# ScalarE's part of a unit's maxima queued three slots later, and whole output units in the last steps of a fused attention and MLP kernel

## Chip, cores and metric

The kernel runs on one core of a Trainium2 chip. The metric is the device time in microseconds of one execution, as the median of several runs. Data is float32; most matrix products are done in float32r with the operands split into a high and a low part.

## What is computed

`x` has 2048 tokens of 576 channels. Two branches read it, and a gate per token mixes them:

```
H = 32; Dh = D // H                       # 18
q, k, v = split(x @ wqkv)
scores = einsum("bhqd,bhkd->bhqk", q, k) * Dh ** -0.5
a = (softmax(scores) @ v, heads joined) @ wo
y = layernorm(x)
b = gelu(y @ w1 + b1) @ w2 + b2           # 576 -> 4608 -> 576
g = sigmoid((x * gate_w).sum(-1))
out = g * a + (1 - g) * b
```

## The kernel before

The order of all instructions is written out by the program itself: a Python planner issues them one by one, each engine runs its own in that order, and semaphores hold an instruction back until its operands are there and its buffer is free.

**Stages.** First come layer norm, transposes and the projections to q, k and v (to about 250 us). Then a long loop does the attention and, between its steps, the MLP. At the end comes the output projection (`out_proj`, line 1297), which also mixes the branches.

**Attention.** A *unit* is a pair of heads and one half of the queries: 32 units. A unit takes 32 *rounds* and 16 *steps*. A round (`s1_round`, products at L227) computes a 128x512 block of scores for each of the two heads, and VectorE takes each row's maximum (L229). When the 32 rounds of a unit are issued, `s1_finish` reduces them to one negative maximum per query (`nm`, VectorE, L238); ScalarE splits it into a rounded part and the rest (`nmh` L239, `nm` L240, `nm2` L241); the function `rows` adds the rest on VectorE (L245), transposes (L246, tile `mr`), and eight small DMAs put the values as two more rows into the tile `qa` of the unit's queries. A step (`s2`) then does, for each half `qb` of the queries, a score product per head with the maximum already subtracted (L307, 56 rows of `qa` and `ka`), and ScalarE takes the exponential (L309, into `p` or `ring`). The two heads' products of a step go into two PSUM banks that only the exponentials free. Rounds have three PSUM banks that VectorE's maxima free in turn. Every second or third step `pv` multiplies the exponentials with v (L335), which closes a *cycle*. The rounds run about 20 steps ahead of the steps: a unit's rounds end four steps before its own first step.

**MLP.** A generator `mlp` yields after every pair of products. `h_pair` does one output of the first matrix (27 pairs of products, L578) and GELU; `out_pair` is one *output unit*: 24 pairs of products with w2 for 128 tokens (48 products, L710), added up on VectorE (L684). `atom` runs the generator up to the next cut that the unit itself has set (a third or so of an output unit), `stretch` for a given time. `fill` is called three times in a cycle of two steps and puts a piece of that work between the attention's products; its products share TensorE with those of a step, since each uses half of the array's rows (`weave`).

**Slots.** `run_due` ends each piece of issue. It counts slots; `defer(n, fn)` runs `fn` n slots later, and this is how small jobs are placed. A step has about four slots.

**Last steps.** The last 20 steps have no rounds left. There `fill` lets `stretch` run the rest of the MLP at a pace worked out from the steps left, and then starts the output projection, 8 products in a gap.

Of the kernel before, what the change touches and what calls it, by code (L numbers as in the profile page):

```python
# [9 lines left out]
F32 = mybir.dt.float32  # L10
F32R = mybir.dt.float32r
AF = mybir.ActivationFunctionType
# [31 lines left out]
GAP = 1130.0  # L44
TOTAL = NB * NG * (G // 2 * 27 * 231 + 8 * 3 * G * 131)
# [7 lines left out]
FIN = NSTEP - 6  # L53
# [7 lines left out]
def gated_mix_kernel(ctx: ExitStack, tc: tile.TileContext, x, wqkv, wo, w1, b1, w2, b2, gate_w, out):  # L61
    nc = tc.nc
# [69 lines left out]
    def dma_r(queue, dst, src):  # L132

        queue.dma_start(dst.bitcast(F32), src)
# [5 lines left out]
    def defer(n, fn):  # L140
        later.append((slot[0] + n, fn))
# [13 lines left out]
    def run_due(ns=SLOT):  # L155

        slot[0] += 1
        now[0] += ns
        if chain and chain[0][0]():
            chain.pop(0)[1]()  # L160
        due = [f for t, f in timed if t <= now[0]]
        timed[:] = [(t, f) for t, f in timed if t > now[0]]
        for f in due:
            f()
        due = [f for s, f in later if s <= slot[0]]
        later[:] = [(s, f) for s, f in later if s > slot[0]]
        for f in due:
            f()
        k = 0
        while k < len(bg):  # L170
            if pool_end[0] - now[0] < bg[k][2] and slot[0] >= bg[k][0]():
                bg.pop(k)[1]()
                k = 0
            else:
                k += 1
# [56 lines left out]
    def s1_finish(u):  # L232

        m4 = M4.pop(u)
        nm = asm.tile([P, 2, 2, 8], F32, name="nm")
        nm2 = asm.tile([P, 2, 2, 8], F32, name="nm2")
        nmh = asm.tile([P, 2, 8], F32R, name="nmh")
        nc.vector.tensor_reduce(nm[:, 0], m4, axis=AX.X, op=ALU.max, negate=True)  # L238
        nc.scalar.activation(nmh, nm[:, 0], AF.Copy)  # L239
        nc.scalar.activation(nm[:, 1], nmh.bitcast(F32), AF.Copy, scale=-1.0)  # L240
        nc.scalar.activation(nm2[:, :, 0, :], nmh.bitcast(F32), AF.Copy)  # L241

        def rows():
            mr = asm.tile([P, 32], F32, name="mr", bufs=1)
            nc.vector.tensor_reduce(nm2[:, :, 1, :], nm.rearrange("p k a b -> p a b k"), axis=AX.X, op=ALU.add)  # L245
            nc.vector.transpose(mr, nm2.rearrange("p a b c -> p (a b c)"))  # L246
            qa = QA[u % 3]
            aside = slot[0] < ybusy[0]

            def store(h, k):  # L250
                r = 64 * h + 54
                c = 32 * k + 16 * h
                dst = qa[r:r + 2, :].rearrange("b (t k n) -> b t k n", k=4, n=32)[:, :, k, :]
                dma_r(nc.scalar if aside else nc.sync, dst, mr[c:c + 16, :])
            for n in range(8):
                if aside:
                    defer(1 + n, lambda n=n: store(*divmod(n, 4)))
                else:
                    store(*divmod(n, 4))
        defer(2 if looped[0] else 8, rows)  # L260

    RING = []

# [105 lines left out]
    rounds = [(u, r) for u in range(NU) for r in range(NR)]  # L369
    rounds.reverse()  # L370

    looped = [False]

    def take_round():
        u, r = rounds.pop()
        head = s1_round(u, r)
        if r == NR - 1:
            defer(1, lambda: s1_finish(u))
        return head
# [425 lines left out]
    stream = [mlp()]  # L805
    spent = [0.0]
# [6 lines left out]
    def atom():  # L813

        while stream:
            try:
                spent[0] += next(stream[0])
            except StopIteration:
                stream.pop(0)
                return 0  # L820
            if cut[0]:
                end, cut[0] = cut[0], 0
                return end
        return 0

    def filler(upto):

        while stream and spent[0] < upto:
            try:
                spent[0] += next(stream[0])  # L830
            except StopIteration:
                stream.pop(0)
            end, cut[0] = cut[0], 0
            if end == 3:
                break
        run_due()


    def stretch(ns):

        upto = spent[0] + ns
        while stream and spent[0] < upto:
            try:
                spent[0] += next(stream[0])
            except StopIteration:
                stream.pop(0)
            end, cut[0] = cut[0], 0
            if end == 3:
                break
# [477 lines left out]
    base = spent[0]  # L1327
    proj = out_proj()
    over = [None]
    bare_at = []  # L1330
    opened = [False]
    at = [0]
    next(proj)
# [3 lines left out]
    def fill(step):  # L1337

        t = spent[0]
        gap = gaps[0]  # L1340
        gaps[0] += 1
        if over[0] is None and rounds:
            behind[0] = base + (TOTAL - KEPT - base) * step / BARE
            ended[0] = atom() == 2
            piece[0] += 1
            run_due(max(spent[0] - t, GAP))
        elif over[0] is None:
            if not bare_at:
                bare_at.extend((gap, spent[0], step))
            g0, s0, n0 = bare_at  # L1350
            stretch(s0 + (TOTAL - s0) * (gap + 1 - g0) / (1.5 * (FIN - n0)) - spent[0])
            run_due(max(spent[0] - t, GAP))
            if not stream:
                stream.append(proj)
                over[0] = gap - (spent[0] == t)
                spent[0] = 0.0
        if over[0] is not None and over[0] < gap:
            filler(PROJ * 122.5 * (gap - over[0]))
            run_due()
# [6 lines left out]
    for u in range(NU):  # L1366
        for kc in range(NT):
            step = u * NT + kc
# [21 lines left out]
            if step - done[0] >= room[0] or room[0] == 3 and ended[0] and step > done[0]:  # L1390
                pv(done[0], step)
                done[0] = step
                piece[0] = 0
                ended[0] = 0
                if extra[0]:
                    next_round()
                    extra[0] -= 1
            else:
                fill(step)
            s2(u, kc, 1, loop_round(), 462.0)  # L1400
            if not (room[0] == 3 and ended[0]):
                fill(step)
# [29 lines left out]
```

## Time and profile before

| | |
|---|---|
| median of 3 runs | 2273.99 us (2273.72 to 2274.64) |
| profiled execution | 2275.26 us |
| its span on the core | 2273.5 us |
| VectorE busy | 1657.7 us, 73% |
| ScalarE busy | 1442.2 us, 63% |
| GpSimd busy | 947.2 us, 42% |
| DMA | 323.62 MB, mean 142 GB/s |

The profile comes from one execution, which took 1.27 us more than the median. All times in it are counted from the start of the span. Each row of the timeline gives start, duration, engine, line, operation, tiles written and read, and in brackets the idle time of the engine before it and what ended that. PE is TensorE, DVE VectorE, ACT ScalarE, POOL GpSimd, SPq the queue of SyncE that issues DMAs. The measured ends of matrix products are modelled.

### The profile page before, as it was taken

Reading aid. Unit: us, or ns where it says so; the run is one execution under the profiler, and the core shown is the slowest. Engines: PE = TensorE matmul, PEld = TensorE weight load, DVE = VectorE, ACT = ScalarE, POOL = GpSimd, SP = SyncE. Lnnn points to the kernel's source line nnn. Section 1 sums busy time; section 2 is a strip of 40 time slices with the busy share of each in tenths; the row PEclk is TensorE's granted clock in tenths of the full one; section 3 lists DMA queues with packets and bytes.
Section 4 is the critical chain, followed back from the end, with each engine's and each line's share of the span. In section 5 each row is a group of like instructions: output and inputs, shape, how many; then the busy total and the mean of one; then the engine's idle time right before and its main releaser. Section 6 shows DMA issues by size and latency. Waiting matters only on the chain. (4 is left out here: it accounts for less than half of the span.)

```text
span 2273.5 us, 51161 instructions
## 1 busy us (share of the span) xinstructions
PE 2238.2 (98%) x20569; PEld 1628.6 (72%) x20569; DVE 1657.7 (73%) x2887; ACT 1442.2 (63%) x2719; POOL 947.2 (42%) x936
## 2 busy tenths in 40 slices
PE   8999999999999999999999999999999999999999
PEld 7878777776777677677667667677766776777669
DVE  5675777777777777777777777777777777777725
ACT  4223777777766666666666666666766666666761
POOL 4002466665654444444444444444624444433510
PEclk9999999999999999999999999999999999999999
DMA  7755645535464434332363323243554332333345
GB/s 242 258 188 182 196 158 157 165 134 189 154 179 181 121 119 121 98 118 98 115 171 127 118 98 121 98 149 111 142 181 128 110 119 93 99 99 112 95 157 192
DMA packets 163411, 323.62 MB, mean 142 GB/s; under 512 B 59838, under 2 KB 86370, under 8 KB 152338
## 3 DMA queue, kind: packets, MB, share of 16 engines
q1 hardware_dynamic: 159174, 313.57, 43.2%
q10 hardware_dynamic: 4000, 6.78, 0.8%
q8 instruction: 162, 2.65, 0.5%
q14 instruction: 75, 0.61, 0.1%
HBM read 229.07 MB, written 95.16 MB: 143 GB/s over the span
## 5 line engine op out<-in xcount | busy, mean ns | idle before, releaser
L229 DVE TENSOR_REDUCE m<-ps 128x1 f32<-128x512 f32 x2048 | 1302.9, 684 | 348.1 <-PE ps L227 310.2
L309 ACT ACTIVATE p<-ps 128x512 f32<-128x512 f32 x1080 | 587.4, 596 | 298.1 <-PE ps L227 193.8
L307 PE MATMUL ps<-qa,ka 56*128 56x512 f32 x2048 | 709.8, 413 | 18.9 <-ACT ring L309 15.2
L309 ACT ACTIVATE ring<-ps 128x512 f32<-128x512 f32 x968 | 525.4, 595 | 263.4 <-PE ps L227 202.2
L227 PE MATMUL ps<-ka,qa 54*128 54x512 f32 x2048 | 649.6, 417 | 3.6 <-DVE m L229 2.5
L710 PE MATMUL ps<-w,hh 64*128 64x288 f32 x4352 | 530.1, 297 | 0.7 <-ACT z L603 0.6
L307 PEld LDWEIGHTS ps<-qa,ka 56*128 56x128 f32 x2048 | 362.8, 185 | 234.5 <-issue 82.1
L578 PE MATMUL ps<-big,w 64*128 64x512 f32 x3888 | 517.4, 392 | 0.1
L180 POOL TENSOR_SCALAR zz<-zz 128x512 f32<-128x512 f32 x272 | 168.3, 619 | 779.9 <-ACT zz L666 749.8
L578 PEld LDWEIGHTS ps<-big,w 64*128 64x128 f32 x3888 | 379.8, 185 | 74.7 <-ACT vt L1016 0.3
L710 PEld LDWEIGHTS ps<-w,hh 64*128 64x128 f32 x4352 | 417.6, 186 | 14.5 <-ACT z L603 1.0
L180 POOL TENSOR_TENSOR zz<-zz,z 128x512 f32<-128x512 f32 x280 | 361.1, 1290 | 34.9 <-ACT zz L668 10.5
L227 PEld LDWEIGHTS ps<-ka,qa 54*128 54x128 f32 x2048 | 339.0, 186 | 34.5 <-DVE m L229 9.4
L710 PE MATMUL ps<-w,hl 64*128 64x288 f32 x2176 | 356.6, 293 | 0.0
L335 PE MATMUL ps<-p,vt 128*32 128x512 f32 x2160 | 266.1, 599 | 0.0
L710 PEld LDWEIGHTS ps<-w,hl 64*128 64x128 f32 x2176 | 241.4, 186 | 1.1
L335 PE MATMUL ps<-ring,vt 128*32 128x512 f32 x1936 | 238.8, 599 | 0.0
L180 POOL TENSOR_TENSOR w<-x,w 128x576 fp32r<-128x576 f32 (+1 forms) x34 | 68.3, 2011 | 282.6 <-ACT w L472 282.5
L180 POOL TENSOR_TENSOR hl<-zz,hh 128x512 fp32r<-128x512 f32 x134 | 174.2, 1300 | 15.3 <-ACT hh L629 4.5
L684 DVE SCALAR_TENSOR_TENSOR x<-ps,x 128x288 f32<-128x288 f32 x268 | 110.1, 452 | 95.4 <-PE ps L710 95.3
L335 PEld LDWEIGHTS ps<-p,vt 128*32 128x32 f32 x2160 | 57.9, 109 | 125.9 <-issue 124.7
L335 PEld LDWEIGHTS ps<-ring,vt 128*32 128x32 f32 x1936 | 52.2, 109 | 112.9 <-issue 112.9
(120 smaller groups left out, 1474.2 us busy)
## 6 DMA issues: line engine op xcount, KB each, us to landing
w<-w_scr SPq DMA_DIRECT2D x54, 1152.0 KB
w<-w_scr SPq DMA_DIRECT2D x108, 576.0 KB
w_scr<-w SPq DMA_DIRECT2D x18, 1152.0 KB
w_scr<-w SPq DMA_DIRECT2D x36, 576.0 KB
qa<-qk_scr SPq DMA_DIRECT2D x192, 72.0 KB
ka<-qk_scr SPq DMA_DIRECT2D x90, 144.0 KB
big<-y_scr SPq DMA_DIRECT2D x48, 256.0 KB
x<-in_B_w_dram SPq DMA_DIRECT2D x34, 288.0 KB
```

The costliest lines, as they stand in the source:

```text
L180: fn(*args, **kw)
L227: nc.tensor.matmul(ps, qa[r0:r0 + 54, t * P:(t + 1) * P], ka[r0:r0 + 54, kb * TB:(kb + 1) * TB], start=True, stop=True)
L229: nc.vector.tensor_reduce(M4[u][:, h, t, kb:kb + 1], ps, axis=AX.X, op=ALU.max)
L307: nc.tensor.matmul(ps, ka[r0:r0 + 56, kc * P:(kc + 1) * P], qa[r0:r0 + 56, qb * TB:(qb + 1) * TB], start=True, stop=True)
L309: nc.scalar.activation(ring(n)[:, qb, h], ps, AF.Exp, scale=SCALE)
L335: nc.tensor.matmul(OB[u][r:r + 32, :], v[:, k, 19 * h:19 * h + 32], ring(c)[:, qb, h, :], start=(k == 0), stop=(k == NT - 1))
L578: nc.tensor.matmul(ps[h], wt[w_][r, c, :], Y[s_][r, c, :], start=(k == 0), stop=(k == 26))
L684: nc.vector.scalar_tensor_tensor(dst, ps[nn][:, :ND], 0.5, b2b[:, cs[nn]] if base else dst, op0=ALU.mult, op1=ALU.add)
L710: mm = nc.tensor.matmul(ps[nn][:, :ND], h_[r, tok], w_[p_][r, cs[nn]], start=(k == 0 or bare and k == 3 * G), stop=(k == 6 * G - 1 or bare ...
```

## The change

There are two parts. In `s1_finish` ScalarE's three instructions go into a function `parts`, which runs three slots later (two before the loop has begun), and `rows` follows it at the distance that it had from `s1_finish` before. In `fill` the branch for steps without rounds goes: while the MLP has work left, every gap takes one piece by `atom`, as in the rest of the loop.

```
         nc.vector.tensor_reduce(nm[:, 0], m4, axis=AX.X, op=ALU.max, negate=True)
-        nc.scalar.activation(nmh, nm[:, 0], AF.Copy)
-        nc.scalar.activation(nm[:, 1], nmh.bitcast(F32), AF.Copy, scale=-1.0)
-        nc.scalar.activation(nm2[:, :, 0, :], nmh.bitcast(F32), AF.Copy)
+
+        def parts():
+            nc.scalar.activation(nmh, nm[:, 0], AF.Copy)
+            nc.scalar.activation(nm[:, 1], nmh.bitcast(F32), AF.Copy, scale=-1.0)
+            nc.scalar.activation(nm2[:, :, 0, :], nmh.bitcast(F32), AF.Copy)
+            defer(2 if looped[0] else 8, rows)
...
-        defer(2 if looped[0] else 8, rows)
+        defer(3 if looped[0] else 2, parts)
...
-        if over[0] is None and rounds:
+        if over[0] is None and stream:
             behind[0] = base + (TOTAL - KEPT - base) * step / BARE
             ended[0] = atom() == 2
             piece[0] += 1
             run_due(max(spent[0] - t, GAP))
-        elif over[0] is None:
-            if not bare_at:
-                bare_at.extend((gap, spent[0], step))
-            g0, s0, n0 = bare_at
-            stretch(s0 + (TOTAL - s0) * (gap + 1 - g0) / (1.5 * (FIN - n0)) - spent[0])
-            run_due(max(spent[0] - t, GAP))
-            if not stream:
-                stream.append(proj)
-                over[0] = gap - (spent[0] == t)
-                spent[0] = 0.0
+        if over[0] is None and not stream:
+            stream.append(proj)
+            over[0] = gap - (spent[0] == t)
+            spent[0] = 0.0
```

No instruction is added or removed. The lines behind the change shift: L307, L309 and L1297 of the program before are L310, L312 and L1300 of the changed one.

ScalarE, at the end of the rounds of unit 26 (near 1844 us), before: `nmh`, `nm`, `nm2` stand behind the exponentials of one step and ahead of the next pair.

```order
L659 ACTIVATE zz<-zz 128x512
L309 ACTIVATE p<-ps 128x512 x8
L309 ACTIVATE ring_2271<-ps 128x512 x4
L309 ACTIVATE ring_2279<-ps 128x512 x2
L239 ACTIVATE nmh<-nm 128x16
L240 ACTIVATE nm<-nmh 128x16
L241 ACTIVATE nm_26835<-nmh 128x2x8
L309 ACTIVATE ring_2279<-ps 128x512 x2
L309 ACTIVATE p<-ps 128x512 x8
```

The same place of the changed program:

```order
L662 ACTIVATE zz<-zz 128x512
L312 ACTIVATE p<-ps 128x512 x8
L312 ACTIVATE ring_2271<-ps 128x512 x4
L312 ACTIVATE ring_2279<-ps 128x512 x4
L312 ACTIVATE p<-ps 128x512 x2
L241 ACTIVATE nmh<-nm 128x16
L242 ACTIVATE nm<-nmh 128x16
L243 ACTIVATE nm_26835<-nmh 128x2x8
L312 ACTIVATE p<-ps 128x512 x6
```

The three instructions have moved behind two more pairs of exponentials.

VectorE at the same place, before: the two instructions of `rows` stand behind the sums of an output unit (L684) and ahead of all eight maxima (L229) of the next cycle.

```order
L684 SCALAR_TENSOR_TENSOR x<-ps,x 128x288 x2
L229 TENSOR_REDUCE m_25952<-ps 128x1 x8
L238 TENSOR_REDUCE nm<-m_25952 128x16
L684 SCALAR_TENSOR_TENSOR x<-ps,x 128x288 x2
L245 TENSOR_REDUCE nm_26835<-nm 128x2x8
L246 STREAM_TRANSPOSE mr<-nm_26835 128x32
L229 TENSOR_REDUCE m_26878<-ps 128x1 x8
L684 SCALAR_TENSOR_TENSOR x<-ps,x 128x288 x2
```

And changed:

```order
L229 TENSOR_REDUCE m_25938<-ps 128x1 x8
L238 TENSOR_REDUCE nm<-m_25938 128x16
L687 SCALAR_TENSOR_TENSOR x<-ps,x 128x288 x2
L229 TENSOR_REDUCE m_26864<-ps 128x1 x4
L248 TENSOR_REDUCE nm_26835<-nm 128x2x8
L249 STREAM_TRANSPOSE mr<-nm_26835 128x32
L229 TENSOR_REDUCE m_26864<-ps 128x1 x4
L687 SCALAR_TENSOR_TENSOR x<-ps,x 128x288 x2
```

`rows` has moved into the middle of the eight maxima.

TensorE in the last cycle of the loop, before, between the last two products with v (L335): products of a step (L307) and of the output projection (L1297).

```order
L335 MATMUL ps<-p,vt_115 32x512 x4
L307 MATMUL ps<-qa_110,ka_28066 128x512 x2
L1297 MATMUL ps<-big 128x288
L1297 MATMUL ps<-wlast,big 128x288
L1297 MATMUL ps<-big 128x288 x6
L307 MATMUL ps<-qa_110,ka_28066 128x512 x2
L1297 MATMUL ps<-big 128x288 x4
L1297 MATMUL ps<-wlast,big 128x288
L1297 MATMUL ps<-big 128x288 x2
L1297 MATMUL ps<-wlast,big 128x288
L307 MATMUL ps<-qa_110,ka_28066 128x512 x2
L1297 MATMUL ps<-big 128x288 x8
```

And changed:

```order
L338 MATMUL ps<-p,vt_115 32x512 x4
L310 MATMUL ps<-qa_110,ka_28066 128x512
L1300 MATMUL ps<-big 128x288
L310 MATMUL ps<-qa_110,ka_28066 128x512
L1300 MATMUL ps<-big 128x288 x7
L310 MATMUL ps<-qa_110,ka_28066 128x512
L1300 MATMUL ps<-wlast,big 128x288
L1300 MATMUL ps<-big 128x288
L310 MATMUL ps<-qa_110,ka_28066 128x512
L1300 MATMUL ps<-big 128x288
L1300 MATMUL ps<-wlast,big 128x288
L1300 MATMUL ps<-big 128x288 x4
```

The two products of a step, which stood together, now have a product or two of the projection between them. Over the cycles without rounds the 288 products of output units that are left come as 40, 40, 42, 40, 40, 40, 40 and 6 to a cycle before, in gaps of 12 or 14, and as 48 in each of six cycles now, in gaps of 14, 16 and 18. Of the 448 products of the projection 64 stand ahead of the last products with v before, in eight gaps (four of them divide a step's pair), and 96 now, in twelve gaps (eight of them divide it).

More of the change, by code (lines that the diff above doesn't have):

```diff
@@ L1329, in gated_mix_kernel @@
     over = [None]
-    bare_at = []
     opened = [False]
```

## The prediction

> **What bounds the kernel now.** I read the page first, then the waits of TensorE in the loop, then the timeline around one of them, then busy time by cycle. On the page the last column of a group is idle time and what ended it.
>
> ```profile
> span 2273.5 us, 51161 instructions
> PE 2238.2 (98%) x20569; PEld 1628.6 (72%) x20569; DVE 1657.7 (73%) x2887; ACT 1442.2 (63%) x2719; POOL 947.2 (42%) x936
> ```
>
> TensorE is busy 98% of the span, so a gain has to come out of its idle time or of products that run slower than they could. Who made it wait between 300 and 2140 us (total, times, longest), and one row of the same view for the whole span:
>
> ```profile
> PE ps L307 <- ACT ring L309: 13.7, 17, 0.8
> PE ps L307 <- ACT p L309: 2.1, 3, 0.8
> ACT nmh L239 <- DVE nm L238: 37.0, 31, 1.7
> ```
>
> Nearly all of it is one kind of wait: a step's product waits for the exponential that frees its bank, 17 times at 0.81 us, and in the second row twice at 0.80 (the third is 0.51). ScalarE in turn waits 31 times, up to 1.7 us, for the maxima of a unit. The timeline at the end of unit 26's rounds ties the two together:
>
> ```profile
> 1840.03 3.88 DVE L229 TENSOR_REDUCE m<-ps 128x1 f32<-128x512 f32 x6 [0.77 <-PE ps L227]
> 1842.87 0.39 PE L307 MATMUL ps<-qa,ka 56*128 56x512 f32 x1
> 1843.94 0.22 DVE L238 TENSOR_REDUCE nm<-m 128x16 f32<-128x64 f32 x1
> 1844.19 0.22 ACT L239 ACTIVATE nmh<-nm 128x16 fp32r<-128x16 f32 x1 [1.72 <-DVE nm L238]
> 1844.67 1.06 ACT L309 ACTIVATE ring<-ps 128x512 f32<-128x512 f32 x2
> 1845.30 0.49 PE L307 MATMUL ps<-qa,ka 56*128 56x512 f32 x1 [0.81 <-ACT ring L309]
> ```
>
> VectorE has six maxima in a row and reaches `nm` at 1843.94. ScalarE stands at `nmh` all that time, and the exponentials of the products of 1842.87, which were ready at about 1843.3, wait behind it until 1844.67. So the next product, 1845.30, waits. What that costs is more than the idle 0.81 us; three cycles with the same products (82 or 83 recorded), each from product with v to product with v, show it, the middle one with the wait:
>
> ```profile
> 1830.31:1837.60 7.29, 7.29 (x83) 5.47 (x81) 5.79 (x11) 4.41 (x10) 6.60 (x7) 1.00 0.03 13
> 1837.60:1846.22 8.62, 7.80 (x83) 5.71 (x81) 6.98 (x16) 5.01 (x12) 0.00 (x0) 1.00 0.01 3
> 1846.22:1853.51 7.29, 7.29 (x82) 5.47 (x81) 5.21 (x9) 4.13 (x9) 0.00 (x0) 1.00 0.14 46
> ```
>
> 8.62 less 7.29 is 1.33 us per unit, and the next cycle gives nothing back.
>
> **The change part by part.** *The wait goes.* `nmh` now comes after two more pairs of exponentials, which places it over the products with v. There ScalarE is idle, as before the first exponentials of the next cycle:
>
> ```profile
> 1846.22 0.64 PE L335 MATMUL ps<-ring,vt 128*32 128x512 f32 x4
> 1848.60 1.09 ACT L309 ACTIVATE p<-ps 128x512 f32<-128x512 f32 x2 [1.68 <-PE ps L227]
> ```
>
> ScalarE's three instructions take 0.48 us from the start of the first to the next exponential (1844.19 to 1844.67) and fit into 1.68, so I cost them at nothing; without that cover each unit would pay up to 0.48. `nm` has then been ready for over 2 us. Gain: 17 + 2 = 19 waits x 1.33 = 25.3 us. The other units end where TensorE did not wait, and give nothing.
>
> *`rows` moves into the maxima.* What is late next is VectorE. The price of `rows` is seen at unit 0, the new place at the cycle after unit 26:
>
> ```profile
> 243.38 0.17 DVE L245 TENSOR_REDUCE nm<-nm 128x16 f32<-128x32 f32 x1
> 243.66 0.21 DVE L246 STREAM_TRANSPOSE mr<-nm 128x32 f32<-128x32 f32 x1
> 243.81 1.29 DVE L229 TENSOR_REDUCE m<-ps 128x1 f32<-128x512 f32 x2
> 1848.64 3.88 DVE L229 TENSOR_REDUCE m<-ps 128x1 f32<-128x512 f32 x6 [1.34 <-PE ps L227]
> 1850.04 1.29 DVE L229 TENSOR_REDUCE m<-ps 128x1 f32<-128x512 f32 x2
> 1850.71 0.58 PE L227 MATMUL ps<-ka,qa 54*128 54x512 f32 x2
> ```
>
> `rows` takes 0.43 us (243.38 to 243.81). It now stands ahead of the third of these six maxima, which starts at 1850.04 and ends near 1850.73 (684 ns). The sixth product of the cycle, the second of the pair at 1850.71, reuses that maximum's bank and starts within 0.1 us of its end: it has no slack. Six maxima in 3.88 us are 0.64 apart, the second starts near 1849.25, VectorE could take the next instruction near 1849.86, and waits about 0.2 us for the third's product. So 0.43 less some 0.2 reach TensorE: I take 0.25 us. It may be 0 where there is more room, and 0.43 with none. The order shows this place at the 19 units above and at four more (2, 9, 16, 23): 23 x 0.25 = 5.8 us lost, between 0 and 9.9.
>
> *Unit 0.* Its `rows` come two slots later, and there the stores are already waited for:
>
> ```profile
> 243.90 5.42 SPq L134 DMA_DIRECT2D qa<-mr  x8
> 250.46 0.79 PE L307 MATMUL ps<-qa,ka 56*128 56x512 f32 x1 [0.70 <-DMA qa<-mr]
> ```
>
> Eight slots lay between 239.06 (its `nm`) and 243.66, some 0.6 us each, and the instructions passed are a pair of maxima, 1.3 us. The wait grows by that: 1.4 us lost, from 0 to 3.
>
> *Stores later in the other units.* The eight stores go out some three slots (a quarter of the step's 7.29 / 2 us each, 2.7 us in all) later. At unit 23, with little room and a load of weights that now goes ahead of them:
>
> ```profile
> 1662.16 5.30 SPq L134 DMA_DIRECT2D qa<-mr  x8
> 1667.56 0.34 SPq L134 DMA_DIRECT2D w<-w_scr  x1
> 1674.83 0.40 PE L307 MATMUL ps<-qa,ka 56*128 56x512 f32 x1
> ```
>
> From the last issue (1667.46) to the first use (1674.83) are 7.4 us; less 2.7 and a landing of 1.1 (unit 0: 249.32 to 250.46) leaves 3.6. Cost nothing; the load's issue takes 0.34 us and waits for nothing in this trace.
>
> *The last steps.* Rows: products with v from the chain of waits, the cycle with 40 output products, a wait and the granted clock (next to last but two) behind it.
>
> ```profile
> 2173.69:2180.11 6.42, 4.01 (x40) 3.42 (x40) 1.00 0.14 53
> 2149.79 0.49 PE L307 MATMUL ps<-qa,ka 56*128 56x512 f32 x1 [1.47 <-ACT ring L309]
> 2152.00:2154.00 2.00, 2.00 (x13) 0.56 (x16) 1.95 (x4) 1.34 (x3) 0.00 (x0) 0.50 0.90 364
> 2142.92 0.64 PE L335 MATMUL ps<-ring,vt 128*32 128x512 f32 x4
> 2152.20 3.24 PE ps L335 x16
> 2160.21 1.85 PE ps L335 x16
> 2200.93 1.85 PE ps L335 x16
> 2210.11 1.85 PE ps L335 x16
> 2217.03 1.85 PE ps L335 x16
> 2218.88 51.28 PE ps L1297 x384
> ```
>
> A cycle of 40 takes 6.42 us, though its output products fill only 4.01: ScalarE's eight exponentials (1.08 a pair) set its pace. Eight more products are four pairs; their price lies between 0, under the exponentials, and 8 x 4.01/40 = 0.80 us, on TensorE. I take 0: 6.4 us for 48. The first two cycles (2142.92 to 2152.20 and to 2160.21: 9.28 and 8.01) have a wait of ScalarE for `nm` too, and GELU's own 1.47 us, after which the clock is halved and the products with v take 3.24 in place of 1.85. With `nm` out of the way I take 8.0 for the first, since all of it starts 0.85 us earlier, and 7.4 for the second, half of the 1.39 that the clock costs. A third takes 7.1 as now, three take 6.4: 41.7 us for the six. Cycles of the projection: 6.92 us with no divided pair (2210.11 to 2217.03), 9.18 with three (2200.93 to 2210.11), so 0.75 for each. Now four cycles with eight divided pairs: 4 x 6.92 + 8 x 0.75 = 33.7. From the first product with v to the last that is 75.4, against 74.1 (2142.92 to 2217.03). The loop thus ends 1.3 us later by itself, but 32 products of the projection are done in it, at 51.28/384 = 0.134 us: 4.3. Net gain 3.0 us, from a loss of 1 to a gain of 6.
>
> *Sum.* 25.3 - 5.8 - 1.4 + 3.0 = 21.1 us off. The profiled execution took 2275.26 (span 2273.5) and would take 2254.2; the median is 1.27 below it, so 2252.9.
>
> The Trainium skill, "TensorE: Matmul & The Clock Gate", section "Why this matters for your kernels", says that TensorE falls back to half clock after an idle window of some 3 us. By that rule the 1.47 us above would not be the cause of the halved clock, it would stay, and the sum would be 0.7 us smaller; the trace here halves after less idle time than the page asks for.
>
> **The rivals.**
> - *`rows` costs nothing*, because VectorE's spare 0.2 us or a later start of the pair covers it: 5.8 us more gain, 2247. Against it stands the sixth product without slack.
> - *The wait moves to VectorE whole*: the sixth product waits each time as the seventh did, 0.8 us and not 0.25: 23 x 0.55 = 12.7 less, 2265.6. It decides if `rows` has itself to wait, for ScalarE's parts; those end over 2 us earlier by the rows above.
> - *The end gives back*: no cover under the exponentials (6 x 0.8 = 4.8) and the last unit's chain, which ends on VectorE at 2245.8 under 208 products and would have only 176, 3.5 to 4.3 us fewer: 2253 + 8 = 2261.
> ```profile
> 2245.14 0.69 DVE L1236 TENSOR_TENSOR big<-x,hh 64x512 fp32r<-64x512 f32 x1 [0.70 <-ACT hh L1230]
> ```
> - *Slower: the maxima land too late.* If the stores queue behind loads, a unit's first product waits. With 3.6 us left at unit 23 the extra delay would have to pass that; at 1 us past it in 31 units the time is 2253 + 31 = 2284. It beats the gain above 0.7 us a unit.
> - *It does not do what it says*: ScalarE stays late for another reason and only the last steps gain: 2271.
>
> The Trainium skill, "DMA: Bandwidth & Descriptors", section "Two DMAs through the same engine are not ordered", says that descriptors of one queue start in order. By that rule the slower rival gets its mechanism at the units where a load is passed. No wait in this trace shows it.
>
> **How the numbers follow.** The forecast, 2249 to 2257, has 0.50; `rows` for nothing 0.22; the end gives back 0.12; the wait moves 0.09; the maxima too late 0.04; not what it says 0.03. The range 2245 to 2262 leaves out the wait that moves and the last two. A change under 0.2% (4.5 us) can't be told from none: faster 0.93, same 0.03, slower 0.04.
>
> **What would show it.** Right: `nmh` idles no more before its start, the 19 cycles take 7.3 to 7.6 us, the waits of L310 for exponentials between 300 and 2140 us fall from 20 to two or three. The step on `rows`: cycles after a unit's end are 0.25 longer than 7.29. The last steps: output cycles near 6.4 with 48 products, and 352 products of the projection behind the last product with v. It is wrong if L310 waits for `qa<-mr` in the loop, or if VectorE's `rows` wait.

## The result, and the profile after

The changed kernel takes 2251.69 us (median of 4 runs, 2250.71 to 2253.85), the kernel before in the same comparison 2274.31 (2273.72 to 2274.8). The ratio is 0.9902 with a 95% interval of 0.9885 to 0.9919: some 22.6 us less. The profiled execution took 2253.85 us. Its span and busy time:

```profile
span 2252.1 us, 51151 instructions
PE 2228.8 (99%) x20569; PEld 1619.0 (72%) x20569; DVE 1651.6 (73%) x2887; ACT 1440.2 (64%) x2719; POOL 947.0 (42%) x936
```

The new lines stand three further down: the score products of a step are L310 (L307 before), the exponentials L312, the products with v L338, the output units L713, the projection L1300. Who made TensorE wait between 300 and 2140 us (total, times, longest):

```profile
PE ps L713 <- DMA w<-w_scr: 6.1, 2, 5.8
PE ps L310 <- ACT ring L312: 0.2, 1, 0.2
```

The 20 waits for exponentials are gone but for one of 0.2 us. In the first row stands a wait for weights, which the prediction does not have. It is not new: the same view of the kernel before, of which the prediction shows two rows, has a third.

```profile
PE ps L710 <- DMA w<-w_scr: 2.3, 1, 2.3
```

The timeline at the end of unit 26's rounds, the same place as shown of before:

```profile
1830.93 1.08 ACT L312 ACTIVATE ring<-ps 128x512 f32<-128x512 f32 x2 [0.82 <-PE ps L310]
1831.59 0.22 DVE L238 TENSOR_REDUCE nm<-m 128x16 f32<-128x64 f32 x1
1831.94 0.39 PE L310 MATMUL ps<-qa,ka 56*128 56x512 f32 x1
1832.37 1.09 ACT L312 ACTIVATE p<-ps 128x512 f32<-128x512 f32 x2 [0.35 <-PE ps L227]
1832.55 1.93 PE L338 MATMUL ps<-ring,vt 128*32 128x512 f32 x16
1833.34 0.22 ACT L241 ACTIVATE nmh<-nm 128x16 fp32r<-128x16 f32 x1
1833.71 0.20 ACT L243 ACTIVATE nm<-nmh 128x16 f32<-128x16 f32 x1
1834.94 1.09 ACT L312 ACTIVATE p<-ps 128x512 f32<-128x512 f32 x2 [1.03 <-PE ps L227]
1836.18 0.18 DVE L248 TENSOR_REDUCE nm<-nm 128x16 f32<-128x32 f32 x1
1836.59 2.44 DVE L229 TENSOR_REDUCE m<-ps 128x1 f32<-128x512 f32 x4
```

The exponentials now go ahead without a stop, and `nmh` (1833.34) starts under the products with v, 1.5 us after `nm` is ready; behind its three instructions ScalarE still sits idle for 1.03 us. `rows` (1836.18) splits the six maxima into two and four. Busy time by cycle, in the order of the cycles shown of before (duration; PE, PEld, DVE, ACT, POOL; clock), then the first two of the last steps and a later one there, and the cycle of the longer wait for weights:

```profile
1817.95:1825.24 7.29, 7.29 (x82) 5.47 (x81) 5.79 (x11) 4.41 (x10) 6.60 (x7) 1.00 0.03 13
1825.24:1832.55 7.31, 7.31 (x83) 5.45 (x81) 6.02 (x12) 4.38 (x9) 0.00 (x0) 1.00 0.01 3
1832.55:1840.00 7.45, 7.45 (x83) 5.37 (x81) 5.97 (x13) 4.88 (x12) 0.00 (x0) 1.00 0.02 3
2123.87:2131.33 7.46, 7.16 (x73) 4.64 (x72) 5.34 (x12) 6.86 (x16) 1.82 (x2) 1.00 0.02 3
2131.33:2137.97 6.64, 6.64 (x73) 4.61 (x73) 6.47 (x14) 5.75 (x12) 0.00 (x0) 1.00 0.01 1
2158.22:2164.78 6.56, 6.56 (x74) 4.61 (x73) 1.65 (x5) 4.35 (x9) 0.74 (x1) 1.00 0.12 45
1161.64:1178.52 16.88, 10.77 (x90) 7.53 (x88) 5.94 (x10) 6.94 (x14) 3.78 (x4) 0.80 0.58 209
```

Unit 26's cycle fell from 8.62 to 7.31 and the next rose from 7.29 to 7.45. The last row is the bad one: the same products take 8.14 us where nothing is late. In the kernel before they took 12.12, with a wait of 2.34:

```profile
1171.89:1184.01 12.12, 9.78 (x89) 6.94 (x88) 5.90 (x10) 6.55 (x14) 3.78 (x4) 0.86 0.66 236
```

TensorE's rows in that cycle of the changed kernel:

```profile
1165.80 0.53 PE L713 MATMUL ps<-w,hh 64*128 64x288 f32 x4 [0.31 <-DMA w<-w_scr]
1172.26 0.60 PE L713 MATMUL ps<-w,w 64*128 64x288 f32 x2 [5.80 <-DMA w<-w_scr]
```

Where the spans' difference of 21.4 us comes from, cycle by cycle: the 20 cycles with a unit's end in which TensorE waited are 26.5 us shorter together (19 of them by 1.30 to 1.46, unit 7's by 1.10), and unit 15's own cycle by 0.4; 16 cycles behind a unit's end are longer by some 0.165, 2.6 in all; unit 0 and the cycle behind unit 7 cost 0.3 each; the longer wait for weights costs 4.8; the last steps are 2.35 shorter (2142.92 to 2273.5 before, 2123.87 to 2252.1 now).

### The profile page after: what moved, and what is told of

The parts are those of the page before. It is cut to its first block, busy times and chain, and to the rows that moved or that the text cites. A ratio compares the mean times of both kernels' runs of the same rounds, so it can differ in the third digit from the quotient of the medians.

```text
span 2252.1 us, 51151 instructions
## 1 busy us (share of the span) xinstructions
PE 2228.8 (99%) x20569; PEld 1619.0 (72%) x20569; DVE 1651.6 (73%) x2887; ACT 1440.2 (64%) x2719; POOL 947.0 (42%) x936
## 4 chain that ended last, share of the span: by engine, by line
PE 95%; DVE 2%; DMA 2%; POOL 1%; ACT 1%; issue 0%; SPq 0%; ACTq 0%; DVEq 0%; POOLq 0%
PE ps L338 20%; PE ps L713 20%; PE ps L581 20%; PE ps L310 14%; PE ps L227 11%; PE ps L990 5%; PE ps L1008 2%; PE ps L1300 1%; PE ps L905 1%; DVE m L229 0%; PE ps L1039 0%; DMA x<-in_A_x_dram 0%; DMA w<-w_scr 0%; DMA qa<-mr 0%; DMA ot_scr<-dn_scr 0%
## 5 line engine op out<-in xcount | busy, mean ns | idle before, releaser
L229 DVE TENSOR_REDUCE m<-ps 128x1 f32<-128x512 f32 x2048 | 1302.3, 684 | 333.5 <-PE ps L227 306.5
L312 ACT ACTIVATE p<-ps 128x512 f32<-128x512 f32 x1080 | 587.0, 596 | 294.3 <-PE ps L227 198.9
L310 PE MATMUL ps<-qa,ka 56*128 56x512 f32 x2048 | 704.7, 411 | 3.2 <-DMA qa<-mr 2.1
L312 ACT ACTIVATE ring<-ps 128x512 f32<-128x512 f32 x968 | 525.8, 596 | 282.0 <-PE ps L227 210.4
L713 PE MATMUL ps<-w,hh 64*128 64x288 f32 x4352 | 530.6, 297 | 1.0 <-ACT z L606 0.6
L310 PEld LDWEIGHTS ps<-qa,ka 56*128 56x128 f32 x2048 | 362.4, 185 | 212.0 <-issue 70.1
L713 PEld LDWEIGHTS ps<-w,hh 64*128 64x128 f32 x4352 | 420.1, 186 | 15.0 <-ACT z L606 1.0
L713 PE MATMUL ps<-w,hl 64*128 64x288 f32 x2176 | 361.6, 292 | 0.0
L338 PE MATMUL ps<-p,vt 128*32 128x512 f32 x2160 | 265.2, 598 | 0.0
L713 PEld LDWEIGHTS ps<-w,hl 64*128 64x128 f32 x2176 | 247.8, 186 | 1.2
L338 PE MATMUL ps<-ring,vt 128*32 128x512 f32 x1936 | 238.3, 598 | 0.0
L338 PEld LDWEIGHTS ps<-p,vt 128*32 128x32 f32 x2160 | 57.9, 109 | 126.9 <-issue 125.7
L338 PEld LDWEIGHTS ps<-ring,vt 128*32 128x32 f32 x1936 | 52.1, 109 | 112.8 <-issue 112.8
```

What stands on the lines that cost most here:

```text
L229: nc.vector.tensor_reduce(M4[u][:, h, t, kb:kb + 1], ps, axis=AX.X, op=ALU.max)
L310: nc.tensor.matmul(ps, ka[r0:r0 + 56, kc * P:(kc + 1) * P], qa[r0:r0 + 56, qb * TB:(qb + 1) * TB], start=True, stop=True)
L312: nc.scalar.activation(ring(n)[:, qb, h], ps, AF.Exp, scale=SCALE)
L338: nc.tensor.matmul(OB[u][r:r + 32, :], v[:, k, 19 * h:19 * h + 32], ring(c)[:, qb, h, :], start=(k == 0), stop=(k == NT - 1))
L713: mm = nc.tensor.matmul(ps[nn][:, :ND], h_[r, tok], w_[p_][r, cs[nn]], start=(k == 0 or bare and k == 3 * G), stop=(k == 6 * G - 1 or bare ...
```

## Experiments

All edits below are against the changed kernel unless they say otherwise. The ratios are to the kernel before in the same comparison.

**Each part alone.** First only `parts` deferred, in the kernel before:

```
+        def parts():
+            nc.scalar.activation(nmh, nm[:, 0], AF.Copy)
...
+            defer(2 if looped[0] else 8, rows)
...
-        defer(2 if looped[0] else 8, rows)
+        defer(3 if looped[0] else 2, parts)
```

> Only the first part of the change: ScalarE's three instructions three slots later, the last steps as before. Theory (the wait for nmh was the bulk): the 19 cycles with a unit's end fall to 7.3 and 8.1 us as in the changed kernel, and the time is 2254 us, the changed kernel's 2251.7 and the 2.35 us that its last steps gained; in the last steps the 1.47 us wait and the halved clock behind it are gone already, which would take some 1.5 us off that and give 2252.5. Rival (the last steps carry more than their spans show): 2258 us or more.

Then only the new branch of `fill`, in the kernel before:

```
-        if over[0] is None and rounds:
+        if over[0] is None and stream:
...
-        elif over[0] is None:
...
-            stretch(s0 + (TOTAL - s0) * (gap + 1 - g0) / (1.5 * (FIN - n0)) - spent[0])
...
+        if over[0] is None and not stream:
```

> Only the second part: whole output units in the last steps, ScalarE's three instructions where they were. Theory: the 20 waits for exponentials between 300 and 2140 us stay, and so do the unit's wait for nmh and the 1.47 us wait in the last steps, or one much like it; the time is 2272 to 2274 us, so 0 to 2 us less than before. Rival (the two parts don't help each other): the whole 2.35 us of the last steps comes from this part, 2272.0. A third way: with more products in a cycle the waiting ones cost more, 2275 to 2276.

Measured: the first part alone 2254.12 us, ratio 0.9909 (0.9892 to 0.9925); the second alone 2272.16, ratio 0.9989 (0.9979 to 0.9998), both against 2274.77. So nearly all comes from the first part. In the last steps the two overlap. From the first cycle without rounds to the end of the span (before 130.58 us, with both parts 128.23), first the run with the first part alone, then the one with the second alone:

```profile
2121.33:2129.56 8.23, 7.04 (x65) 4.21 (x65) 6.81 (x10) 7.36 (x17) 7.03 (x6) 1.00 0.01 3
2129.56:2136.65 7.09, 6.78 (x65) 4.19 (x64) 7.02 (x15) 5.58 (x12) 0.00 (x0) 1.00 0.01 1
2121.33:2250.00 128.67, 123.40 (x991) 94.58 (x990) 60.06 (x112) 60.18 (x112) 14.18 (x14) 1.00 0.47 154
```

```profile
2142.42:2150.29 7.87, 7.26 (x74) 4.66 (x73) 5.35 (x12) 7.22 (x17) 1.81 (x2) 1.00 0.07 10
2142.42:2270.80 128.38, 123.76 (x991) 94.34 (x990) 57.45 (x112) 59.61 (x112) 13.58 (x14) 1.00 0.49 164
```

Each alone removes the halved clock there and saves 1.91 and 2.20 us; together they save 2.35. With the second part alone no wait like that of 1.47 us is left (the longest is 0.37), so its theory was wrong on that. On top of the first part whole output units are worth 0.44 us, which is less than the runs can tell. The median of 2254 of the first part alone is the first number that its theory named, but not for its reason, which had 2.35 us for the last steps. Against the kernel before in its own comparison the first part alone gains 20.7 us and both parts 22.6; the intervals of the two ratios overlap.

**`rows` at another place.** One slot after `parts`:

```
-            defer(2 if looped[0] else 8, rows)
+            defer(1 if looped[0] else 8, rows)
```

> The changed kernel with rows one slot after parts, not two: on VectorE it then stands behind the first two maxima of the next cycle, beside the products with v, and no longer between the fourth and fifth. Theory (rows delays the sixth product's bank): the 16 cycles of 7.45 and 8.3 us fall back to 7.29 and 8.14, 16 x 0.165 = 2.6 us less than 2251.7, so 2249. The stores of unit 15 go out a slot earlier as well, which may take up to 0.7 us off the wait for w<-w_scr. Rival (any place among the maxima costs the same, since VectorE gives nothing back within a cycle): 2251.7. A second rival (the longer cycles come from the eight DMA issues of that stretch): they stay at 7.45, 2251.7 or 0.5 less.

Measured: 2248.8 us (2247.76 to 2249.86), ratio 0.9885 (0.987 to 0.9899). VectorE at unit 26 and the two cycles that were 7.31 and 7.45 (a timeline, then busy time by cycle):

```profile
1828.63 1.28 DVE L229 TENSOR_REDUCE m<-ps 128x1 f32<-128x512 f32 x2
1829.83 0.18 DVE L248 TENSOR_REDUCE nm<-nm 128x16 f32<-128x32 f32 x1
1830.68 3.88 DVE L229 TENSOR_REDUCE m<-ps 128x1 f32<-128x512 f32 x6 [0.37 <-PE ps L227]
```

```profile
1820.98:1828.26 7.28, 7.28 (x83) 5.45 (x81) 6.01 (x12) 4.34 (x9) 0.00 (x0) 1.00 0.01 3
1828.26:1835.56 7.30, 7.30 (x83) 5.46 (x82) 6.11 (x13) 4.80 (x12) 0.00 (x0) 1.00 0.02 4
```

`rows` now stands in a gap that VectorE has anyway (0.37 us are left of it), the six maxima are in one row again, and all 12 cycles of 7.45 are back at 7.27 to 7.31. The four of 8.3 stayed at 8.30 to 8.32, and that is the check on it: at units 2, 9, 16 and 23 `rows` comes behind four of the next maxima with either number. So the first theory holds for the place, and the size of the gain in the cycles is 12 x 0.165 = 2.0 us, not 2.6. The cycle behind unit 7 fell too, from 11.84 to 11.58. Most of the rest of the profiled execution's gain is in the wait for the weights, which was 2.96 us in it.

**The wait for the weights.** SyncE's own waits from 1140 to 1182 us, before and after (total, times, longest):

```profile
SPq L134 <- DMA qa<-mr: 17.4, 5, 13.4
```

```profile
SPq L134 <- DMA qa<-mr: 20.3, 4, 16.0
```

In both kernels the queue of SyncE stood up to 13.4 and 16.0 us before the loads of w2, waiting for the stores of unit 15, which go out on ScalarE's queue, one in each slot (`aside`). The program shows why they depend on each other. DMAs of both queues share eight completion semaphores in turn, and nearly every one waits for the one that used its semaphore before it. ScalarE's first two stores and SyncE's first two loads, in the order of the changed kernel, with the semaphores that each waits for (`DMAHW0_49` to `DMAHW7_49` are the eight):

```
714 L134 DMA qa_109<-mr 2x8x32 [waits DMAHW7_49,DMAHW2_49,DVE_49]
715 L134 DMA qa_109<-mr 2x8x32 [waits DMAHW3_49,DMAHW0_49]
...
779 L134 DMA w_16554<-w_scr 128x1152 [waits DMAHW2_49,PE_49]
780 L134 DMA w_16556<-w_scr 128x1152 [waits DMAHW3_49,PE_49]
```

The trace has the same chain in time. The packets of the first three stores end at 1159.98, 1160.70 and 1163.70 us; the first three loads are issued at 1160.39, 1161.08 and 1164.30. The third store, issued at 1160.21, moves its first packet only at 1163.50, behind packets of the first load. So each load waits for a store, and from the third on the stores wait among the loads. The test sends unit 15's stores by SyncE's queue, like those of all other units but unit 7, which puts them behind the loads:

```
-            aside = slot[0] < ybusy[0]
+            aside = slot[0] < ybusy[0] and u != 15
```

> The changed kernel with the eight stores qa<-mr of unit 15 on SP's queue, as in the other units, behind the four loads w<-w_scr, and not on ScalarE's queue. Theory (the loads are held back by the landing of the stores: SP stands 16.0 us in a wait for qa<-mr, and the change made the stores three slots later): the loads go out near 1144 us, the wait of 5.80 + 0.31 us of L713 for w<-w_scr is gone, and the time is 2246 us (down to 5 us less than the changed kernel's 2251.7 in the same runs, since not all of its runs may wait that long). Rival (the transfers are slow there, whatever the issue): a wait of 2 us or more stays, 2249 to 2251.7. Second rival (the stores now come too late behind the loads of y): L310 waits for qa<-mr, 2252 or more.

The same edit in the kernel before:

> The kernel before with one edit: unit 15's stores on SP's queue behind the loads w<-w_scr. Theory (the loads have been held back by the stores' landing in the kernel before too): the wait of 2.34 us of L307's neighbour L710 goes, with the halved clock behind it; its cycle falls from 12.12 to 8.14 us, so 4.0 less than 2274.5, 2270.5. Rival (only the later stores of the change make the loads wait; before, they waited for memory): 2274.5, with the wait still there.

Measured: 2245.84 us (2245.34 to 2246.73), ratio 0.9872 (0.9857 to 0.9887), for the changed kernel; 2269.75, ratio 0.9979 (0.997 to 0.9987) against 2275.23, for the kernel before. SyncE's queue and the cycle in question with the edit in the changed kernel, then that cycle in the kernel before with it:

```profile
1150.18 1.91 SPq L134 DMA_DIRECT2D w<-w_scr  x4
1159.60 5.30 SPq L134 DMA_DIRECT2D qa<-mr  x8
```

```profile
1163.12:1171.26 8.14, 8.14 (x90) 5.69 (x89) 5.82 (x10) 6.69 (x14) 3.82 (x4) 1.00 0.42 147
```

```profile
1170.53:1178.66 8.13, 8.13 (x90) 5.69 (x88) 5.82 (x10) 6.69 (x14) 3.81 (x4) 1.00 0.42 147
```

The loads go out at 1150, ten us earlier than in the changed kernel, and both kernels lose the whole wait: 16.88 and 12.12 became 8.14 and 8.13. It was there before the change, at less than half the size in these profiles. The timed runs do not show that difference: the edit takes 5.9 us off the median of the changed kernel and 5.5 off that of the kernel before (4.0 were forecast; the interval is 3.0 to 6.8).

**Did the three slots lengthen it?** Unit 15 alone keeps its old place for `parts`, with the stores still on ScalarE's queue:

```
-        defer(3 if looped[0] else 2, parts)
+        if u == 15:
+            parts()
+        else:
+            defer(3 if looped[0] else 2, parts)
```

> The changed kernel with ScalarE's three instructions of unit 15 alone at their old place, so that its stores go out three slots earlier, still on ScalarE's queue. Theory (the three slots are what lengthened the wait for w<-w_scr): the wait falls from 5.80 + 0.31 to about 2.3 to 3.0 us and its cycle from 16.88 to some 12.1, with 0.4 us back at unit 15's own cycle (11.5 for 11.14): 2248 to 2249.5. Rival (the wait is longer since TensorE gets there sooner, or by chance of the transfers): it stays at 5 to 6 us, 2251.7.

Measured: 2251.0 us (2249.05 to 2253.02), ratio 0.9901 (0.9886 to 0.9916). In its profile the wait is 2.8 us, as the theory has it, yet the median moved by 0.7 only, so both kernels were profiled again.

> The changed kernel a second time, for the wait of L713 for w<-w_scr near 1170 us, which was 5.80 + 0.31 us in its first profile. Theory (three slots are what lengthened it, as in the first run with unit 15's three instructions at their old place, 2.22 + 0.56): 5 us or more again. Rival (it varies from execution to execution, with the landing of the stores among the packets of the loads): anything from 2.5 to 6 us.

> The changed kernel with ScalarE's three instructions of unit 15 at their old place, a second time. Theory (the three slots lengthen the wait): 2.3 to 3 us for w<-w_scr again. Rival (it varies from execution to execution, as the spread of that kernel's times, 2249.05 to 2253.02, lets one think): in one of the two repeats 4 us or more.

> The changed kernel a third time, as its second. Theory: 5 us or more. Rival: the three waits of this kernel lie more than 2 us apart.

TensorE's wait for `w<-w_scr` in these three, in this order (L716 is L713 with the edit's lines):

```profile
PE ps L713 <- DMA w<-w_scr: 5.1, 2, 4.1
```

```profile
PE ps L716 <- DMA w<-w_scr: 2.4, 1, 2.4
```

```profile
PE ps L713 <- DMA w<-w_scr: 5.5, 2, 5.1
```

Three executions of the changed kernel: 6.1, 5.1 and 5.5 us, cycles of 16.88, 16.46 and 15.43. Two with unit 15 early: 2.8 and 2.4, cycles of 11.41 and 12.18. Two runs shown above belong here as well: with the first part alone unit 15 is as late as in the changed kernel, and with the second part alone it is early. Their rows, in this order:

```profile
PE ps L713 <- DMA w<-w_scr: 4.2, 2, 3.8
PE ps L710 <- DMA w<-w_scr: 3.0, 2, 2.3
```

Their cycles took 14.25 and 13.04 us. With the kernel before (2.3, 12.12) that makes four late executions of 14.25 to 16.88 us and four early ones of 11.41 to 13.04. The two groups don't touch, so in the profiles the three slots do lengthen this cycle, by 1.2 to 5.5 us, of which unit 15's own cycle takes back 0.4. The times (2258.01, 2250.11 and 2252.94 in the repeats) do not show that size cleanly; their scatter is as large, and why the medians of the timed runs differ by only 0.7 us (1.6, each counted from the kernel before in its own comparison) stays open.

**The edits together.** Unit 15's stores on SyncE's queue, `rows` one slot after `parts`, and `parts` at once before the loop:

```
-        defer(3 if looped[0] else 2, parts)
+        if looped[0]:
+            defer(3, parts)
+        else:
+            parts()
```

> Three edits on the changed kernel together: unit 15's stores on SP's queue, rows one slot after parts, and before the loop ScalarE's three instructions at once as in the kernel before (rows eight slots after them). Theory (they are independent): from the 2245.84 us of the first edit alone, 2.0 less (12 cycles of 7.45 back at 7.29, as the run of rows alone showed), and 1.1 less at unit 0, where the two waits for qa<-mr fall from 2.1 to the 1.0 us of the kernel before: 2242.7. Rival (the halved clock behind unit 0's wait is what costs, and it stays): 2243.8. Second rival (rows gained mostly by sending unit 15's stores earlier, which the first edit has already taken): 2244.7.

Measured: 2241.35 us (2240.73 to 2242.74), ratio 0.9856 (0.9843 to 0.987), the fastest version here, 33.9 us under the kernel before in the same comparison (2275.23). At unit 0 the wait for `qa<-mr` is back at the 0.7 us of the kernel before. The theory had 3.1 us less than the 2245.84 of the first edit alone, and 4.5 came out. The profiles place the surplus at unit 0: the clock behind it was halved for 3.41 us and not for 6.83, and the cycle in which unit 1's rounds end began at 294.92 us, 2.7 earlier than with the first edit alone, where 1.1 was forecast. Then the last of it, with unit 0's `rows` four slots after `parts` and not eight:

> The three edits together, and unit 0's rows four slots after ScalarE's three instructions in place of eight, so that its stores go out some 2 us earlier. Theory: the waits of L310 for qa<-mr near 250 us are gone, 1.0 us less than the three edits alone; with 0.74 us of idle time left there in place of 1.7, the halved clock behind it (6.83 us in the record) goes as well, some 3 us more: 2238.5 to 2239. Rival (the clock is halved there for another reason): 2241.7. Second rival (something else is late there next, the exponentials or the maxima): 2242.7.

Measured: 2241.62 us (2240.71 to 2242.32), no gain. TensorE's waits from 248 to 260 us in that run:

```profile
PE ps L313 <- ACT p L315: 0.3, 1, 0.3
PE ps L227 <- DVE m L229: 0.3, 1, 0.3
PE ps L716 <- DVE z L608: 0.2, 1, 0.2
```

The wait for the stores is gone, but an exponential takes its place with 0.3 us, and the clock was halved for 6.83 us all the same, against 3.41 in the run with eight slots. The theory that less idle time there would keep the clock up fell.

## Why the prediction was right, and where not

The sum for the profiled execution, 2254.2 us, came out at 2253.85. The term that carries it, the wait, was right, but that the sum is this close is luck: some 5.9 us came out better than forecast (`rows` 3.2, units 7 and 15 1.5, unit 0 1.1, the 19 waits 0.1) and 5.8 worse (the loads behind unit 15's stores 4.8, the last steps 0.65, the cycle behind unit 7 0.3).

- *The wait goes*: right in mechanism and size. 19 cycles gave 25.4 us where 25.3 stood. Unit 7's gave 1.1 more; its wait of 0.51 us had been left out of the count. `nmh` idles before none of its 32 starts now. The sign of 7.3 to 7.6 us held for 15 of the 19 cycles; the other four, from 9.47 to 9.53 before, take 8.14 to 8.18.
- *`rows` moves into the maxima*: right in mechanism, shown by the run that moves it, but the term of 23 x 0.25 = 5.8 was mis-sized. It was 16 cycles of 0.165, 2.6 us; that run moves it in 12 of them. Seven units cost nothing: behind three of them comes a cycle with 54 products of the MLP's first matrix (some 11.15 us), behind four one with 28 (some 7.23), and both kinds stayed as long as they were. Why they cover `rows` was not tested.
- *Unit 0*: the waits for `qa<-mr` rose from 0.7 to 2.1 us, as the 1.4 forecast said (TensorE, 248 to 260 us, changed kernel):

```profile
PE ps L310 <- DMA qa<-mr: 2.1, 2, 1.3
```

Yet the cycle in which unit 1's rounds end began only 0.3 us later than before (296.33 for 296.04). That small cost is luck of this pair of executions: the clock behind unit 0 was halved for 6.83 us in both. In three other executions with unit 0's old order (the second part alone, the kernel before with unit 15's stores moved, the three edits together) it was halved for 3.41 us, and that cycle began at 294.9 to 295.0. In all eight with the changed order it was halved for 6.83, and the cycle began at 296.3 to 297.6. Against those three the step costs 1.3 to 2.7 us.
- *Stores later in the other units*: this is the step that failed. It looked at the first use of the stores and at SyncE's queue at unit 23, found room, and cost them at nothing. What hangs on a store is also every later DMA that waits for its semaphore. At unit 15, where the stores go out on ScalarE's queue and not on the SyncE queue that the step looked at, those were the loads of w2, and they cost 4.8 us in this pair of executions (2.1 to 4.8 in four with unit 15 late). The rows that tell it, 17.4 us of SyncE waiting for `qa<-mr` and TensorE's 2.3 us for `w<-w_scr`, stood in the trace of before. The slower rival had the queues the wrong way round: the loads waited for the stores, and one unit paid, not 31.
- *The last steps*: forecast 3.0, measured 2.35, with first cycles of 7.46, 6.64 and 7.13 where 8.0, 7.4 and 7.1 stood. The four projection cycles took 34.6 where 33.7 stood. The three equal cycles took 6.55 to 6.57 with 48 products, so eight more products cost some 0.13 us, near the 0 that was taken and far from the bound of 0.80: they lie under the exponentials. But most of this gain belongs to the first part, which already takes the wait and the halved clock away.
- *The clock*: the place that was halved in the kernel before after 1.47 us idle kept its full clock once the wait was 0.22. In the run with the first part alone it kept it after 1.11 us. The rule of the Trainium skill, "TensorE: Matmul & The Clock Gate", section "Why this matters for your kernels" (some 3 us of idle time), by which the halved clock would have stayed there, does not fit that place. It gets support from one run: 2.2 us for the weights passed at full clock. In the repeat of that same kernel 2.4 us did not. The waits here do not give one threshold.

## To carry to other kernels

When a small DMA is moved, look for what waits for its completion semaphore as well as for who reads its data: the waits of the issuing queue, sorted by what ended them, show it in one row, and idle time of that queue is free only until a load behind it is needed. When an instruction is queued later to clear a head-of-line wait, place it over work in which its engine is idle, and do the same for what follows it; one slot decided 2 us here. Before a difference of one profile is explained, see whether other executions with the same order show it: the 0.3 us at unit 0 did not last. Sum the gains by cycle, since two edits that remove the same wait each look worth the whole of it when run alone.

## What was not expected of the hardware

- Small stores that share the DMA engines with large loads land late: in the changed kernel the store issued at 1160.21 us, with a load issued 0.18 us behind it, moved its first packet 3.3 us later, the two before it within 1.3.
- The granted clock differs between executions with the same waits. In the changed kernel's second profile it was halved for 10.24 us from 2195.52 on, behind a wait of 0.64 us that left it at full speed in the first (0.65) and third; that execution took 2258.01 us. Rows of the same stretch in both, second profile first:

```profile
2195.00:2200.00 5.00, 5.00 (x14) 3.08 (x13) 2.33 (x5) 2.59 (x5) 0.00 (x0) 0.55 1.04 397
2200.00:2205.00 5.00, 5.00 (x20) 2.34 (x23) 2.48 (x4) 1.87 (x4) 0.00 (x0) 0.50 0.10 37
```

```profile
2195.00:2200.00 5.00, 5.00 (x28) 3.09 (x31) 3.37 (x6) 3.63 (x7) 0.00 (x0) 1.00 1.05 399
2200.00:2205.00 5.00, 5.00 (x40) 3.93 (x33) 3.19 (x7) 0.72 (x2) 0.00 (x0) 1.00 0.23 69
```
- The halved stretches in the records last 3.41, 6.83 or 10.24 us, multiples of the same 3.41, apart from the one that runs past the end of each.
